# Two homes for the transposed activations, and queries asked for ahead of keys and values, in a fused sparse attention and feed-forward kernel

## The chip, the cores and the metric

The kernel runs on one core of a Trainium2 chip. The metric is device time in microseconds of one execution; before the change its median is 812.19 us over 3 runs (811.87 to 813.76).

## The reference

Block-sparse attention (4 batches, 8 heads, 768 positions, head size 64, blocks of 32) is followed by a layer norm and a feed-forward layer with a residual:

```
scores = q k^T / 8, masked by block: neighbours, first and last block, 3 sampled blocks per query block
attn   = softmax(scores) v                      (first and last query block see all keys)
x      = attn, heads side by side               (4 x 768 rows of 512)
xn     = (x - mean) / sqrt(var + 1e-6) * g
out    = x + relu(xn w1) w2                     (w1 512 x 2048, w2 2048 x 512)
```

## The kernel before

The 3072 rows are 24 tiles of 128, six for each batch, in the order t = 1, 2, 3, 0, 4, 5. Each tile with t > 0 is one job of kind N (four query blocks, each with 8 key blocks) with two visits, one for each half of the heads. Tile t = 0 holds the four edge blocks: a job H with one visit and a job D (two blocks that see all keys) with four. So a batch has 15 visits, and `s` counts the visits of the whole program.

At each step `s` the loop writes, in this order: `scores` of this visit (TensorE, line 203, into `ps`), `biggest` (VectorE, lines 236 to 239), `attn_v` and `evict` of the visit before (line 266 into `pv`, lines 295 to 312), `softmax` (ScalarE, line 246), then a list of tasks (loads for the next job, `turn` of this visit at line 256, pieces of weight preparation in the first steps, `norms`) with feed-forward matmuls spread between them by a budget (`run`). Every engine executes in the order written. There is no scheduler behind it.

The loads of the next job are written at the first visit of the present one and all go through SyncE's queue (SP), which issues in order and waits in order:

- `keys` of an N job: one DMA for the neighbour blocks (line 144, 768 KB), then twelve gathers of one sampled block each (line 153, 64 KB each), three for each of the four query blocks; D: two halves (line 134, 768 KB each). Two buffers `ks` by turns.
- `values`: lines 180 and 188 on SP (D: line 176, 1560 KB) and gathers by index on GpSimd's queue (line 192). Two buffers `vs` by turns.
- `load_q` (line 171, 256 KB): the queries of the next tile, from a table of tasks by step, so behind all of the next job's keys and values.

A matmul of `scores` for an N visit needs the tile's queries and the three gathers of its query block; the loop runs over two head pairs, and over the four blocks within each.

The rows of a tile are normed (`norm_a`: lines 319 to 327, giving the fp16 parts `xh` and `xl`), and two DMA transposes on SP (`norm_b`, lines 331 and 332) bring them into `xth` and `xtl`, from where the up projection (`ffn`, line 349 into `pu`) reads them. There is one `xth` and one `xtl`, with room for the two tiles of a unit (the first and the last unit have one tile). So a unit's transposes wait until the unit before has done its last up matmul (`up_done`). The down projection is line 373 (`pd`), its eviction line 379. In the first visits VectorE, ScalarE and GpSimd also split the weights into two fp16 parts (`split_w`, lines 402 to 413), 4 pieces a step.

Of the kernel before, what the change touches and what calls it, by code (L numbers as in the profile page):

```python
# [10 lines left out]
F16 = mybir.dt.float16  # L11
# [14 lines left out]
def sparse_attention_moe(  # L26
# [13 lines left out]
    nc = tc.nc  # L40
    P = 128
# [3 lines left out]
    CT, FT = DM // P, DF // P  # L45
# [4 lines left out]
    const = ctx.enter_context(tc.tile_pool(name="const", bufs=1))  # L50
# [6 lines left out]
    def ring(name, n, shape, dtype):  # L57
        return [const.tile(shape, dtype, name=f"{name}{i}") for i in range(n)]
# [12 lines left out]
    xn_s = const.tile([P, DM], F32, name="xn")  # L71
    xh_s = ring("xh", 2, [P, DM], F16)
    xl_s = ring("xl", 2, [P, DM], F16)
    xth = const.tile([P, CT, 2 * P], F16, name="xth")
    xtl = const.tile([P, CT, 2 * P], F16, name="xtl")
    hh_s = const.tile([P, FT * 2 * P], F16, name="hh")
    hl_s = const.tile([P, FT * 2 * P], F16, name="hl")
    ot_s = ring("ot", 2, [P, DM], F32)
# [7 lines left out]
            name=nc.get_next_instruction_name(), act_func_set_id=ACT_SET, ins=[], outs=[]  # L86
# [146 lines left out]
    def biggest(vi):  # L233
        n, w = vi.shape
        st = vi.st = sm.tile([P, 8], F32, tag="st", name=f"st{vi.i}")
        nc.vector.tensor_reduce(out=st[:, 0:n],  # L236
                                in_=vi.ps[:, 0 : n * w].rearrange("p (h k) -> p h k", k=w),
                                axis=AX.X, op=ALU.max, negate=True)
        nc.vector.tensor_scalar(out=st[:, 4 : 4 + n], in0=st[:, 0:n], scalar1=0.125,
                                scalar2=None, op0=ALU.mult)  # L240
# [75 lines left out]
    def norm_a(t):  # L316
        st = sm.tile([P, 10], F32, tag="ln", name=f"ln{t.n}")
        x, xn, xh, xl = t.x, xn_s, xh_s[t.n % 2], xl_s[t.n % 2]
        nc.vector.bn_stats(st[:, 0:6], x)
        nc.vector.bn_aggr(st[:, 6:8], st[:, 0:6])  # L320
        nc.scalar.activation(st[:, 8:9], st[:, 7:8], AF.Ln, bias=eps)
        nc.scalar.activation(st[:, 9:10], st[:, 8:9], AF.Exp, scale=-0.5)
        nc.vector.scalar_tensor_tensor(out=xn, in0=x, scalar=st[:, 6:7], in1=g_sb,
                                       op0=ALU.subtract, op1=ALU.mult)
        nc.scalar.activation(xn, xn, AF.Copy, scale=st[:, 9:10])
        nc.scalar.copy(xh, xn)
        nc.gpsimd.tensor_sub(xl, xn, xh)  # L327

    def norm_b(t):
        s = slice(t.pos * P, (t.pos + 1) * P)  # L330
        nc.sync.dma_start_transpose(out=xth[:, :, s], in_=xh_s[t.n % 2])
        nc.sync.dma_start_transpose(out=xtl[:, :, s], in_=xl_s[t.n % 2])

    def ffn(u):
        n = len(u.tiles) * P
        hh = hh_s[:, 0 : FT * n].rearrange("p (f n) -> p f n", n=n)
        hl = hl_s[:, 0 : FT * n].rearrange("p (f n) -> p f n", n=n)
        step = 512 // n
        c1 = 109 if n == 256 else 84
        for f in range(0, FT, step):  # L340
            while any((1, x // 2) not in split for x in range(f, f + step)):
                yield -1
            ph = ps_f.tile([P, 512], F32, tag="pf", name=f"pu{u.i}_{f}")
            for j in range(step):
                fs = slice((f + j) * P, (f + j + 1) * P)
                m = 0
                for w, x in ((w1h, xth), (w1l, xth), (w1h, xtl)):
                    for ct in range(CT):
                        nc.tensor.matmul(ph[:, j * n : (j + 1) * n], w[:, ct, fs], x[:, ct, 0:n],  # L349
                                         start=m == 0, stop=m == 3 * CT - 1,  # L350
                                         skip_group_check=True)
                        m += 1
                        if m < 3 * CT:
                            yield c1
                if j < step - 1:
                    yield c1
            dh = hh[:, f : f + step, :].rearrange("p f n -> p (f n)")
            dl = hl[:, f : f + step, :].rearrange("p f n -> p (f n)")
            nc.scalar.activation(dh, ph, AF.Relu)  # L359
            nc.vector.scalar_tensor_tensor(out=dl, in0=ph, scalar=0.0, in1=dh,  # L360
                                           op0=ALU.max, op1=ALU.subtract)
            if f + step == FT:
                u.up_done = True
            yield c1
        for t in u.tiles:
            ts = slice(t.pos * P, (t.pos + 1) * P)
            po = ps_f.tile([P, 512], F32, tag="pf", name=f"pd{t.n}")
            m = 0
            for f in range(FT):
                while (2, f) not in split:  # L370
                    yield -1
                for x, w in ((hh, w2h), (hl, w2h), (hh, w2l)):
                    nc.tensor.matmul(po, x[:, f, ts], w[:, f, :], start=m == 0,  # L373
                                     stop=m == 3 * FT - 1)
                    m += 1
                    if m < 3 * FT:
                        yield 215
            ot = ot_s[t.n % 2]
            nc.vector.scalar_tensor_tensor(out=ot, in0=po, scalar=1.0 / (SW1 * SW2), in1=t.x,  # L379
                                           op0=ALU.mult, op1=ALU.add)  # L380
            nc.gpsimd.dma_start(out[t.b, t.t], ot)
            t.done = True
            yield 215
# [44 lines left out]
    tiles, units, visits = [], [], []  # L428
# [5 lines left out]
    while n < len(tiles):  # L434
        k = 1 if n == 0 or n == len(tiles) - 1 else 2
        u = SimpleNamespace(i=len(units), tiles=tiles[n : n + k], up_done=False, gen=None)
# [32 lines left out]
    def at(step, fn, *args):  # L469
        todo.setdefault(step, []).append((fn, args))  # L470
# [19 lines left out]
        at(3, load_w2, i, nc.gpsimd)  # L490
    for i in range(16):
        at(4 + i // 4, split_w2, i)
    for t in tiles[1:]:
        at(tiles[t.n - 1].visits[0].i, load_q, t.n)
    for b in range(1, B):
        at(tiles[6 * b - 2].visits[0].i, load_kg, b)

    queue, nextu, s = [], 0, 0
# [14 lines left out]
    def norms():  # L513
        for t in tiles:
            if t.ready and t.normed is None and (t.n < 2 or tiles[t.n - 2].spread is not None):
                norm_a(t)
                t.normed = s
            if t.normed is not None and t.spread is None:
                if t.u.i == 0 or units[t.u.i - 1].up_done:
                    norm_b(t)  # L520
                    t.spread = s

    while s < NV + LAG + 2 or queue or nextu < len(units):
        assert s < NV + 60
        vi = visits[s] if s < NV else None
        pvi = visits[s - LAG] if 0 <= s - LAG < NV else None
        if vi:
            scores(vi)
            biggest(vi)
        if pvi:  # L530
            t = pvi.tile
            if pvi is t.visits[0]:
                assert t.n < NX or tiles[t.n - NX].done
            attn_v(pvi)
            evict(pvi)
            if pvi is t.visits[-1]:
                t.ready = True
        if vi:
            softmax(vi)
        while nextu < len(units) and units[nextu].at <= s:  # L540
            u = units[nextu]
            if any(t.spread is None or t.spread >= s for t in u.tiles):
                break
            u.gen = ffn(u)
            u.left = 192 * (84, 109)[len(u.tiles) - 1] + 48 * 215 * len(u.tiles)
            queue.append(u)
            nextu += 1
        budget = 0
        if queue:
            left = sum(u.left for u in queue)  # L550
            budget = left / (max(1, units[nextu].at - s) if nextu < len(units) else 1)
        tasks = [(fn, args) for fn, args in todo.pop(s, [])]
        if vi:
            nxt = jobs[vi.job.i + 1] if vi is vi.job.visits[0] and vi.job.i + 1 < len(jobs) else None
            pre = []
            if nxt:
                gen = keys(nxt)
                pre = [(next, (gen, 0)), (values, (nxt,))] + [(next, (gen, 0))] * 6
            tasks = pre + tasks
            if queue:  # L560
                k = len(tasks) // 2
                tasks = tasks[:k] + [(turn, (vi,))] + tasks[k:]
            else:
                tasks = [(turn, (vi,))] + tasks
        tasks.append((norms, ()))
        for fn, args in tasks:
            run(budget / (len(tasks) + 1))
            fn(*args)
        if queue:
            want = sum(u.left for u in queue) - (left - budget)  # L570
            run(want)
        norms()
        s += 1

# [50 lines left out]
```

## Time and profile before

| | |
|---|---|
| median of 3 runs | 812.19 us (811.87 to 813.76) |
| profiled execution, its own time | 817.5 us |
| its span | 815.7 us |
| TensorE busy (matmul) | 717.9 us, 88% |
| TensorE weight loads | 483.8 us, 59% |
| VectorE / ScalarE / GpSimd busy | 314.2 / 278.3 / 210.8 us |
| DMA moved | 132.16 MB, 162 GB/s over the span |

The profile's page divides the span into 40 slices of 20.4 us. TensorE is below nine tenths of each slice up to about 160 us and at 9 nearly everywhere after it. So the time before 160 us is read by what VectorE, ScalarE, GpSimd and the DMA queues do there, and the time after it by the few places in which TensorE stands still.

### The profile page before, as it was taken

The numbers are of one execution on the slowest core, as the hardware profiler recorded it, in microseconds if no ns is written. First come the engines' busy times: TensorE is split into PE (matmuls) and PEld (weight loads), VectorE is DVE, ScalarE is ACT, GpSimd is POOL, SyncE is SP. The second block draws the span as 40 slices with busy tenths as digits, with TensorE's granted clock in tenths as the row PEclk, the third lists the DMA queues.
The fourth block names the chain that finished last, engine by engine and source line by source line (L and its number), as shares of the span: only waits on it lengthen the run. The fifth ranks groups of instructions, "written<-read, shape, count | busy, mean of one in ns | idle before, by whom it ended". The sixth has DMA issues, their size and how long they took to land.

```text
span 815.7 us, 21773 instructions
## 1 busy us (share of the span) xinstructions
PE 717.9 (88%) x9344; PEld 483.8 (59%) x9344; DVE 314.2 (39%) x618; ACT 278.3 (34%) x553; POOL 210.8 (26%) x236
## 2 busy tenths in 40 slices
PE   0545565999999999999999999989999999989997
PEld 0234432675685774765774856755866846756764
DVE  2577877334242341443341432333432332342211
ACT  0356454233343341342342431343432422333200
POOL 5276547121412103023230202023321020200000
PEclk9966786799999999999999999999999999999999
DMA  8997789138938439168947367168757194261000
GB/s 332 260 322 194 279 259 248 53 89 201 259 107 223 123 103 282 32 158 224 229 97 185 99 198 207 41 161 233 215 138 185 33 277 128 70 141 40 14 27 14
DMA packets 109792, 132.16 MB, mean 162 GB/s; under 512 B 34561, under 2 KB 80897, under 8 KB 108673
## 3 DMA queue, kind: packets, MB, share of 16 engines
q1 hardware_dynamic: 96848, 83.92, 40.0%
q0 software_dynamic: 12416, 46.51, 17.7%
q8 instruction: 74, 1.21, 0.6%
q10 hardware_dynamic: 432, 0.34, 0.1%
q14 instruction: 22, 0.17, 0.1%
HBM read 118.15 MB, written 6.29 MB: 153 GB/s over the span
## 4 chain that ended last, share of the span: by engine, by line
PE 55%; issue 20%; DMA 13%; POOL 5%; SPq 4%; DVE 2%; ACT 1%; POOLq 0%
PE pu L349 24%; PE pd L373 16%; PE ps L203 7%; DMA vs<-v 6%; PE pv L266 5%; PE pt L256 4%; DMA ks<-kT 4%; SPq L153 3%; DMA q<-qT 2%; POOL w2l L413 2%; POOL vs L192 1%; DVE ot L404 1%; POOL xl L327 1%; DMA samp<-sampled 1%; POOL ks L168 0%
## 5 line engine op out<-in xcount | busy, mean ns | idle before, releaser
L246 ACT ACTIVATE p<-ps,st 128x256 f32<-128x256 f32 (+1 forms) x192 | 83.3, 510 | 273.4 <-DVE rs L295 164.8
L349 PEld LDWEIGHTS <-w1h 128*128 128x128 f16 x1664 | 152.7, 99 | 18.6 <-issue 0.3
L373 PE MATMUL pd<-w2l,hh 128*128 128x512 f16 x384 | 147.5, 384 | 8.2 <-POOL w2l L413 4.5
L373 PE MATMUL pd<-w2h,hh 128*128 128x512 f16 x384 | 147.3, 384 | 3.1 <-ACT w2h L412 3.1
L373 PE MATMUL pd<-w2h,hl 128*128 128x512 f16 x384 | 147.5, 384 | 0.0
L360 DVE SCALAR_TENSOR_TENSOR hl<-pu,hh 128x512 f16<-128x512 f32 x96 | 66.4, 692 | 181.1 <-ACT hh L359 180.2
L373 PEld LDWEIGHTS <-hh 128*128 128x128 f16 x768 | 75.4, 99 | 94.5 <-issue 13.2
L203 PE MATMUL ps<-ks,q 64*32 64x256 f32 (+1 forms) x1664 | 83.5, 420 | 47.6 <-DMA ks<-kT 26.2
L349 PE MATMUL pu<-xth,w1l 128*128 128x256 f16 (+1 forms) x832 | 120.6, 266 | 0.0
L349 PE MATMUL pu<-xth,w1h 128*128 128x256 f16 (+1 forms) x832 | 120.6, 266 | 0.0
L349 PE MATMUL pu<-xtl,w1h 128*128 128x256 f16 (+1 forms) x832 | 120.5, 265 | 0.1
L236 DVE TENSOR_REDUCE st<-ps 128x4 f32<-128x1024 f32 (+1 forms) x60 | 69.1, 1151 | 122.6 <-PE ps L203 122.6
L192 POOL DMA_INDIRECT vs<-v,rows x88 | 87.9, 998 | 99.1 <-PE pv L266 60.5
L359 ACT ACTIVATE hh<-pu 128x512 f16<-128x512 f32 x96 | 57.4, 598 | 125.0 <-PE pu L349 110.9
L256 PE MATMUL pt<-id_sb,p 128*128 128x128 f32 x448 | 67.5, 293 | 28.4 <-ACT p L246 28.4
L203 PEld LDWEIGHTS ps<-ks,q 64*32 64x32 f32 x1664 | 34.8, 110 | 85.6 <-issue 75.0
L257 ACT COPY pt<-pt 128x512 f32<-128x512 f32 x120 | 62.1, 564 | 64.7 <-PE pt L256 56.9
L349 PEld LDWEIGHTS <-w1l 128*128 128x128 f16 x832 | 78.2, 99 | 8.5
L256 PEld LDWEIGHTS pt<-id_sb,p 128*128 128x128 f32 x448 | 54.9, 149 | 40.1 <-ACT p L246 33.4
L379 DVE SCALAR_TENSOR_TENSOR ot<-pd,x 128x512 f32<-128x512 f32 x24 | 16.6, 690 | 156.5 <-PE pd L373 156.5
L266 PEld LDWEIGHTS pv<-vs,pt 128*32 128x32 f32 x3584 | 56.5, 112 | 32.9 <-issue 24.1
L266 PE MATMUL pv<-vs,pt 128*32 128x65 f32 x3584 | 67.9, 225 | 5.1 <-issue 2.9
(75 smaller groups left out, 416.4 us busy)
## 6 DMA issues: line engine op xcount, KB each, us to landing
ks<-kT SPq DMA_DIRECT2D x28, 768.0 KB
ks<-kT SPq DMA_DIRECT2D x264, 64.0 KB
vs<-v SPq DMA_DIRECT2D x20, 780.0 KB
vs<-v SPq DMA_DIRECT2D x4, 1560.0 KB
q<-qT SPq DMA_DIRECT2D x24, 256.0 KB
out<-ot POOLq DMA_DIRECT2D x24, 256.0 KB
vs<-v SPq DMA_DIRECT2D x16, 260.0 KB
w2h<-w POOLq DMA_DIRECT2D x4, 1024.0 KB
```

Of the source, the lines that this page charges most:

```text
L153: nc.sync.dma_start(kv[:, gg, r, :], src[:, bass.ds(reg[NR * gg + r], 1), :] .rearrange("p o e -> p (o e)"))
L192: nc.gpsimd.indirect_dma_start(out=vs[:, 2 * gg, :], out_offset=None, in_=src, in_offset=bass.IndirectOffsetOnAxis(ap=rows[:, i : i + 1], ...
L203: nc.tensor.matmul(ps[32 * part : 32 * part + 32, col : col + n], lhs[64 * row : 64 * row + 64], rhs[64 * row : 64 * row + 64], start=True ...
L236: nc.vector.tensor_reduce(out=st[:, 0:n], in_=vi.ps[:, 0 : n * w].rearrange("p (h k) -> p h k", k=w), axis=AX.X, op=ALU.max, negate=True)
L246: nc.scalar.activation(p_s[:, hs], vi.ps[:, hs], AF.Exp, bias=vi.st[:, 4 + h : 5 + h], scale=0.125)
L256: nc.tensor.transpose(pt[:, k - lo, :], p_s[:, k * P : (k + 1) * P], id_sb)
L257: nc.scalar.copy(dst[:, lo:hi, :], pt[:, 0 : hi - lo, :])
L266: nc.tensor.matmul(pv[32 * row : 32 * row + 32, 65 * col : 65 * col + 65], pt[:, ch, 32 * row : 32 * row + 32], vs[:, vv, 65 * e : 65 * e ...
L349: nc.tensor.matmul(ph[:, j * n : (j + 1) * n], w[:, ct, fs], x[:, ct, 0:n], start=m == 0, stop=m == 3 * CT - 1, skip_group_check=True)
L359: nc.scalar.activation(dh, ph, AF.Relu)
L360: nc.vector.scalar_tensor_tensor(out=dl, in0=ph, scalar=0.0, in1=dh, op0=ALU.max, op1=ALU.subtract)
L373: nc.tensor.matmul(po, x[:, f, ts], w[:, f, :], start=m == 0, stop=m == 3 * FT - 1)
```

## The change

Three things change. `xth` and `xtl` become two each, used by turns of the unit. The condition on a tile's transposes is relaxed accordingly: they are written once the unit two before (no longer the one before) has done its up matmuls. And `load_q` leaves the table of tasks: it is written ahead of the next job's keys and values, when that job is the first of its tile.

```
-    xth = const.tile([P, CT, 2 * P], F16, name="xth")
-    xtl = const.tile([P, CT, 2 * P], F16, name="xtl")
+    xth_s = ring("xth", 2, [P, CT, 2 * P], F16)
+    xtl_s = ring("xtl", 2, [P, CT, 2 * P], F16)
...
-        nc.sync.dma_start_transpose(out=xth[:, :, s], in_=xh_s[t.n % 2])
-        nc.sync.dma_start_transpose(out=xtl[:, :, s], in_=xl_s[t.n % 2])
+        nc.sync.dma_start_transpose(out=xth_s[t.u.i % 2][:, :, s], in_=xh_s[t.n % 2])
+        nc.sync.dma_start_transpose(out=xtl_s[t.u.i % 2][:, :, s], in_=xl_s[t.n % 2])
...
     def ffn(u):
         n = len(u.tiles) * P
+        xth, xtl = xth_s[u.i % 2], xtl_s[u.i % 2]
...
-    for t in tiles[1:]:
-        at(tiles[t.n - 1].visits[0].i, load_q, t.n)
...
-                if t.u.i == 0 or units[t.u.i - 1].up_done:
+                if t.u.i < 2 or units[t.u.i - 2].up_done:
...
-                pre = [(next, (gen, 0)), (values, (nxt,))] + [(next, (gen, 0))] * 6
+                pre = [(load_q, (nxt.visits[0].tile.n,))] if nxt.visits[0] is nxt.visits[0].tile.visits[0] else []
+                pre += [(next, (gen, 0)), (values, (nxt,))] + [(next, (gen, 0))] * 6
```

Where it moves instructions is seen on SP. `DMAHW` names are the eight semaphores that SP's DMAs use by turns; a wait on PE, Activation or Pool is one on a compute engine. First, SP between the H job's loads and the next N job's in the third batch, about 455 to 487 us in the trace. Before:

```order
L171 DMA q1_89<-qT 128x512 [waits DMAHW6_49]
L331 DMA_TRANSPOSE xth_100<-xh1_97 128x4x128 [waits DMAHW7_49,PE_49,Activation_49]
L332 DMA_TRANSPOSE xtl_101<-xl1_99 128x4x128 [waits DMAHW0_49,PE_49,Pool_49]
L134 DMA ks0_79<-kT 128x1536 [waits DMAHW1_49]
L176 DMA vs0_83<-v2 128x6x520 [waits DMASW7_49,DMASW6_49,DMAHW2_49,DMASW5_49,PE_49]
L134 DMA ks0_79<-kT 128x1536 [waits DMAHW3_49]
L171 DMA q0_88<-qT 128x512 [waits DMAHW4_49]
L331 DMA_TRANSPOSE xth_100<-xh0_96 128x4x128 [waits DMAHW5_49,Activation_49]
L332 DMA_TRANSPOSE xtl_101<-xl0_98 128x4x128 [waits DMAHW6_49,Pool_49]
L144 DMA ks1_80<-kT 128x4x384 [waits DMAHW7_49]
```

Now:

```order
L331 DMA_TRANSPOSE xth1_101<-xh1_97 128x4x128 [waits DMAHW7_49,Activation_49]
L332 DMA_TRANSPOSE xtl1_103<-xl1_99 128x4x128 [waits DMAHW0_49,Pool_49]
L134 DMA ks0_79<-kT 128x1536 [waits DMAHW1_49,PE_49]
L176 DMA vs0_83<-v2 128x6x520 [waits DMASW7_49,DMASW6_49,DMAHW2_49,DMASW5_49,PE_49]
L134 DMA ks0_79<-kT 128x1536 [waits DMAHW3_49]
L331 DMA_TRANSPOSE xth1_101<-xh0_96 128x4x128 [waits DMAHW4_49,Activation_49]
L332 DMA_TRANSPOSE xtl1_103<-xl0_98 128x4x128 [waits DMAHW5_49,Pool_49]
L171 DMA q0_88<-qT 128x512 [waits DMAHW6_49]
L144 DMA ks1_80<-kT 128x4x384 [waits DMAHW7_49]
```

The transposes stand where they stood, but the first pair no longer waits for TensorE; the D job's keys behind them now carry that wait, for an older visit's scores. The query load has moved behind the second pair, directly ahead of its own tile's keys.

Second, SP at the end of that same kind of round, after the twelve gathers of one N job and before the loads of the next (about 370 us in the trace). Before:

```order
L171 DMA q1_89<-qT 128x512 [waits DMAHW3_49]
L161 DMA kg0_81<-kT 128x2x128 [waits DMAHW4_49]
L331 DMA_TRANSPOSE xth_100<-xh1_97 128x4x128 [waits DMAHW5_49,PE_49,Activation_49]
L332 DMA_TRANSPOSE xtl_101<-xl1_99 128x4x128 [waits DMAHW6_49,PE_49,Pool_49]
L144 DMA ks0_79<-kT 128x4x384 [waits DMAHW7_49,PE_49]
L180 DMA vs0_83<-v2 96x4x520 [waits DMAHW0_49,PE_49]
L188 DMA vs0_83<-v2 32x4x520 [waits DMAHW1_49]
```

Now:

```order
L161 DMA kg0_81<-kT 128x2x128 [waits DMAHW4_49]
L331 DMA_TRANSPOSE xth1_101<-xh1_97 128x4x128 [waits DMAHW5_49,Activation_49]
L332 DMA_TRANSPOSE xtl1_103<-xl1_99 128x4x128 [waits DMAHW6_49,Pool_49]
L171 DMA q0_88<-qT 128x512 [waits DMAHW7_49,PE_49]
L144 DMA ks0_79<-kT 128x4x384 [waits DMAHW0_49]
L180 DMA vs0_83<-v2 96x4x520 [waits DMAHW1_49,PE_49]
L188 DMA vs0_83<-v2 32x4x520 [waits DMAHW2_49]
```

The queries of the coming tile (`q1_89`) are gone from here: they went out ahead of its keys, one round earlier. Those of the tile after it (`q0_88`) stand ahead of line 144 instead of behind the next twelve gathers.

Third, SP in the first batch, ahead of the first D job (about 82 to 110 us). Before:

```order
L171 DMA q1_89<-qT 128x512 [waits DMAHW0_49]
L134 DMA ks0_79<-kT 128x1536 [waits DMAHW1_49,PE_49]
L176 DMA vs0_83<-v0 128x6x520 [waits DMASW2_49,DMASW1_49,DMAHW2_49,DMASW0_49,PE_49]
L134 DMA ks0_79<-kT 128x1536 [waits DMAHW3_49]
L171 DMA q0_88<-qT 128x512 [waits DMAHW4_49]
L331 DMA_TRANSPOSE xth_100<-xh1_97 128x4x128 [waits DMAHW5_49,PE_49,Activation_49]
L332 DMA_TRANSPOSE xtl_101<-xl1_99 128x4x128 [waits DMAHW6_49,PE_49,Pool_49]
```

Now:

```order
L331 DMA_TRANSPOSE xth1_101<-xh1_97 128x4x128 [waits DMAHW1_49,Activation_49]
L332 DMA_TRANSPOSE xtl1_103<-xl1_99 128x4x128 [waits DMAHW2_49,Pool_49]
L134 DMA ks0_79<-kT 128x1536 [waits DMAHW3_49,PE_49]
L176 DMA vs0_83<-v0 128x6x520 [waits DMASW2_49,DMASW1_49,DMAHW4_49,DMASW0_49,PE_49]
L134 DMA ks0_79<-kT 128x1536 [waits DMAHW5_49]
```

Here, and only here, a pair of transposes has come ahead of loads that it used to follow.

ScalarE executes in the same order. On TensorE a few `turn` and `scores` groups of the H and D visits move by 2 to 5 down matmuls. On VectorE and GpSimd, once in each of the last three batches, the eviction and store of a finished down projection come ahead of a tile's norm instead of behind it.

## Rows read from the trace of the kernel before

**Rows 1.** The page: span, and TensorE's busy tenths in 40 slices.

```profile
span 815.7 us, 21773 instructions
...
PE   0545565999999999999999999989999999989997
```

**Rows 2.** Windows: length, busy us of PE, PEld, DVE, ACT, POOL, granted clock, DMA share, GB/s.

```profile
40.00:60.00 20.00, 10.46 (x200) 7.61 (x200) 15.31 (x17) 10.69 (x17) 14.24 (x12) 0.60 0.91 318
...
100.00:120.00 20.00, 13.16 (x183) 8.46 (x185) 13.89 (x24) 10.97 (x21) 8.82 (x10) 0.82 0.82 245
...
380.00:400.00 20.00, 18.29 (x276) 11.46 (x275) 4.81 (x11) 6.29 (x15) 10.18 (x12) 1.00 0.95 243
...
480.00:500.00 20.00, 19.55 (x167) 9.93 (x166) 3.04 (x9) 4.57 (x9) 6.76 (x8) 1.00 1.09 325
```

**Rows 3.** Waits: engine and line, what for, us in total, times, longest us.

```profile
PE ps L203 <- DMA q<-qT: 16.6, 5, 8.1
```

**Rows 4.** Timeline of TensorE, scores of N visits: start, us, then idle before and releaser.

```profile
50.01 2.30 PE L203 MATMUL ps<-ks,q 64*32 64x256 f32 x32 [8.06 <-DMA q<-qT]
...
72.72 2.29 PE L203 MATMUL ps<-ks,q 64*32 64x256 f32 x32 [4.18 <-DMA q<-qT]
...
196.45 1.43 PE L203 MATMUL ps<-ks,q 64*32 64x256 f32 x32 [1.19 <-issue]
...
372.90 1.52 PE L203 MATMUL ps<-ks,q 64*32 64x256 f32 x32 [1.14 <-DMA q<-qT]
...
393.00 1.43 PE L203 MATMUL ps<-ks,q 64*32 64x256 f32 x32 [1.21 <-DMA q<-qT]
...
529.03 1.09 PE L203 MATMUL ps<-ks,q 64*32 64x256 f32 x32
...
551.10 1.52 PE L203 MATMUL ps<-ks,q 64*32 64x256 f32 x32 [2.04 <-DMA q<-qT]
...
728.56 1.52 PE L203 MATMUL ps<-ks,q 64*32 64x256 f32 x32 [1.87 <-issue]
```

**Rows 5.** Timeline of TensorE: first D visits of three batches, and an H step's attn_v.

```profile
311.10 1.49 PE L203 MATMUL ps<-ks,q 64*32 64x512 f32 x16 [1.29 <-DVE ot L379]
...
475.51 1.11 PE L266 MATMUL pv<-vs,pt 128*32 128x65 f32 x64
...
488.42 1.49 PE L203 MATMUL ps<-ks,q 64*32 64x512 f32 x16 [0.46 <-DMA ks<-kT]
...
666.47 1.50 PE L203 MATMUL ps<-ks,q 64*32 64x512 f32 x16 [1.20 <-DMA ks<-kT]
```

**Rows 6.** Chain that ended last: start, us from issue to landing, transfer.

```profile
369.80 2.86 DMA q<-qT
...
477.95 10.33 DMA ks<-kT
...
677.84 3.34 DMA ks<-kT
```

**Rows 7.** SP's own waits, the one on line 331.

```profile
SPq L331 <- PE pu L349: 110.6, 8, 28.9
```

**Rows 8.** Timeline of SP, third batch: last H query load, transposes, D values.

```profile
454.95 1.31 SPq L171 DMA_DIRECT2D q<-qT  x1
474.19 1.22 SPq L331 DMA_TRANSPOSE xth<-xh  x1
...
477.52 0.38 SPq L176 DMA_DIRECT2D vs<-v  x1
```

**Rows 9.** Timeline of GpSimd: the step that makes xl, first and third batch.

```profile
95.54 1.15 POOL L327 TENSOR_TENSOR xl<-xn,xh 128x512 f16<-128x512 f32 x1
...
462.95 1.15 POOL L327 TENSOR_TENSOR xl<-xn,xh 128x512 f16<-128x512 f32 x1 [10.30 <-ACT xh L326]
```

**Rows 10.** Timeline of VectorE: row maxima of the visits at 50 and 73 us.

```profile
52.34 1.22 DVE L236 TENSOR_REDUCE st<-ps 128x4 f32<-128x1024 f32 x1 [4.11 <-PE ps L203]
...
75.06 1.23 DVE L236 TENSOR_REDUCE st<-ps 128x4 f32<-128x1024 f32 x1 [1.82 <-PE ps L203]
```

## Prediction

> **What bounds the kernel now.** I read the page first, to find the stretches with different limits, then the windows, then TensorE's waits by line, then TensorE's timeline at each of those waits, and last SP's queue and the chain of waits, to see what landed late and why. The page's slices show two stretches [rows 1]: until about 160 us TensorE is far from full; after it, TensorE is full but for short stops. In the first stretch the other engines and the DMA queues are busy: between 40 and 60 us VectorE works 15.3 us of 20 and the DMA share is 0.91 [rows 2]. In the second, an idle microsecond of TensorE is a microsecond of the kernel, unless the same transfer makes it wait again soon after. So I look for idle time of TensorE after 160 us, and for idle time of VectorE before it.
>
> TensorE waited 16.6 us in five places for the query load alone [rows 3]; two more such places are put down to "issue". They are the first visits of N tiles: at 50.01 and 72.72 us in the first stretch, at 196.45, 372.90, 393.00, 551.10 and 728.56 in the second [rows 4]. The reason is the place of the load in SP's queue: it is the last of the tile's transfers. At 369.80 it is issued after twelve gathers, lands 2.86 us later [rows 6], and the scores start 0.24 us after that [rows 4]. The second kind of stop is the first visit of a D job, 1.29, 0.46 and 1.20 us [rows 5]. There the D keys come late because SP stands on a pair of transposes that waits for the up projection of the unit before: nothing is issued from 454.95 to 474.19 [rows 8], and line 331 waited 110.6 us for TensorE in 8 places [rows 7]. The three D-job stops are the ones where a late load stands behind such a wait.
>
> **The sum, term by term.**
>
> Term A, queries first, after 160 us. Nothing is added or taken away: 24 query loads move ahead of their tile's keys and values, and the gathers are issued about when they were, since the values load ahead of them still waits for TensorE. What must land last is now the twelfth gather. The five stops cost 1.19 + 1.14 + 1.21 + 2.04 + 1.87 = 7.45 us idle, and the visits after them run 1.43 to 1.52 us where an undisturbed one runs 1.09, together 7.42 - 5 x 1.09 = 1.97 more [rows 4]. So 9.42 us is the ceiling. The floor comes from the gather's landing. A gather issued into a crowded queue at 677.84 landed in 3.34 us, against the query load's 2.86, and it is issued some 0.4 us (one issue) sooner [rows 6], so it may land no earlier than the queries did. Even then TensorE gains: the loop over four query blocks runs twice, and the last block's keys are first needed after 6 of 16 groups. What is left after the landing is 10/16 of 1.09 to 1.52, that is 0.68 to 0.95 us, where all of 1.52 was left: at least 0.55 us a stop. I take 1.0 a stop, between 0.55 and the 1.6 to 2.4 of single stops, since it is nearest to the row with the shorter flight, 2.86. The stops at 372.90 and 393.00 hang on one run of transfers with a DMA share of 0.95 [rows 2], so they don't add up: the second gains what the first did, and 256 KB that no longer lie in that run, 0.8 us at 325 GB/s. That is 1.8 us for both. With 1.0 at 196.45, 1.5 at 551.10 (a weaker second stop follows it) and 1.0 at 728.56, A is 5.3 us; bounds 2.2 (four independent places x 0.55) and 9.4.
>
> Term B, transposes no longer waiting, after 160 us. In the third batch the pair can go when the tile's `xl` is made, 462.95 + 1.15 = 464.1 [rows 9], instead of 474.19. The first half of the D keys, 768 KB, then goes at about 467. The D values wait for the H step's attn_v, 475.51 + 1.11 = 476.6, 0.9 us before they now go [rows 5, 8], and the second half goes behind them. So 2328 KB instead of 3096 KB lie between 477 and D's scores. The second half now takes 10.33 us from issue to landing [rows 6]; three quarters of that is 7.8, landing at about 485, and the scores are due at 488. All three stops go: 2.95 us. I take 2.8; bounds 0 (the D1 stop at 311.10 is put down to VectorE, and the others may be) and 2.95. The other waits of line 331 are worth nothing: no stop follows them. What gets later: in the last three batches the next tile's pair now stands behind the eviction of a down projection that ends about when D's scores start (488.42), not close behind the H step (476.6) [rows 5], and SP's loads of the next N tile stand behind that pair: up to 12 us later. Their first reader is the visit at 529.03 [rows 4], 40 us on: cover enough, and if it were gone the price would be up to those 12 us a batch.
>
> Term C, before 160 us. VectorE's chain of weight splits and row maxima sets the pace there. It idles 4.11 us for the scores at 50 us and 1.82 us for those at 73 [rows 10]. At 50 us the clock is 0.60 of full [rows 2] and the scores take 2.30; with queries first 10/16 of them, 1.4, is left after the last landing, which saves 0.9, and up to 0.4 for the earlier issue. The next job's values go out behind that visit's attn_v, so its saving is passed on; at 73 us the same 1.3 is saved again, and VectorE's idle 1.82 covers it. That is 2.6 at most by this reckoning, 3.5 if the landings come earlier. Against it stands the one place where transposes have come ahead of loads: the first D keys, now behind `xl` at 95.54 + 1.15 [rows 9]. 768 KB move into a stretch with 245 GB/s at a share of 0.82 [rows 2], which can cost up to 3.1 us or, with that room, nothing. I take C as 2.0; bounds -3.1 and 3.5.
>
> Sum: 5.3 + 2.8 + 2.0 = 10.1 us. The profiled execution took 817.5 us, so 807.4; it is 5.3 us above the median of 812.19, on which the same gain gives **802.1 us**. With all ceilings it is 812.2 - 15.9 = 796.3.
>
> **The rivals.**
>
> Queue-bound: the order in the queue is indifferent. For it speaks the share of 0.95 between 380 and 400 us [rows 2]: if the queue is full, the last byte lands when it did, whichever transfer it belongs to, and a bunch of gathers arriving together leaves no part of a visit to run ahead. A and C are then nothing, B stays: 812.2 - 2.9 = 809.3 us. Against it speaks the load at 369.80, which took 2.86 us for 256 KB: that is a short flight, not a queue. The Trainium skill has this rule ("DMA: Bandwidth & Descriptors", Two DMAs through the same engine are not ordered: descriptors within one queue of an engine start in order but are pipelined); the row at 369.80 agrees only in part, since SP's issue and not the queue sets the time there.
>
> Nothing moves: the transposes stand in SP's queue where they stood, only their wait is gone, and SP meets the next wait of the same time (for `xl`, for the older visit's scores, for attn_v). With the gathers landing as late as the queries did, each stop stays under another name: 812 us. Against it: the waits that come next are over 10 us (464.1) and 0.9 us (476.6) earlier by the rows above.
>
> Slower: the first D keys, behind the transposes of tile 1, arrive after their visit is due. The row maximum of that visit then comes late, VectorE's last four weight splits stand behind it, and TensorE's full stretch begins later. The price is 3.1 us of transfer, and if A and B gave nothing the kernel would take 812.2 + 3.1 = 815.3. It decides only where A and B fail together, since their floors of 2.2 and 2.9 outweigh it; the share of 0.82 speaks against it too.
>
> **How the numbers follow.** The forecast, A to C at about these sizes, has a chance of 0.74; queue-bound 0.13; nothing moves 0.07; slower 0.06. A measurement of this kernel can tell about 0.3%, 2.4 us, from no change. The forecast is faster by more than that, and so is the queue-bound case in most of its width (I give 0.1 of 0.13 to faster): faster 0.84, same 0.10, slower 0.06. The range goes from the ceilings, 796, to the queue-bound case, 809.5; it leaves out the last two rivals and a little of the others.
>
> **What would show each step.** TensorE's waits by line should have no entry "ps from DMA q" of more than 1 us after the first visits; what is left of the stops should be put down to `ks`. The first D visits should start without idle time, with the first half of the D keys issued about 10 us ahead of the D values. SP's line 331 should wait for ScalarE or GpSimd and no longer for TensorE. VectorE's row maxima near 50 and 73 us should come 1 to 3 us sooner, and TensorE's full stretch should begin about 2 us sooner. The prediction is wrong if the stops in the N tiles keep their 1 to 2 us with `ks` as the releaser, if a new stop appears at the N tile after a D job, or if the D visit of the first batch waits for its keys.

## The result, and the profile after

The changed kernel takes 798.69 us (median of 6 runs, 798.03 to 799.43), the kernel before, run beside it, 812.21 (809.59 to 813.76). The ratio is 0.9837, with a 95 % interval of 0.9821 to 0.9852: 13.5 us faster. On two more chips the same pair gave 0.988 (0.9854 to 0.9907) and 0.9854 (0.9815 to 0.9894), so about 11 us there. The forecast was 802.1, the range 796.0 to 809.5.

The page of the profiled execution after: span, and TensorE's busy tenths in 40 slices.

```profile
span 796.1 us, 21782 instructions
...
PE   0476474899999999999999999999999999999997
```

The slices with 8 after 160 us [rows 1] are gone. TensorE's waits show why. These are the two entries that its scores (line 203) have left: engine, line, what for, us in total, times, longest.

```profile
PE ps L203 <- DMA ks<-kT: 30.1, 7, 22.7
...
PE ps L203 <- issue: 0.5, 2, 0.2
```

There is no entry for the query load, which stood with 16.6 us [rows 3]; the keys stand with 30.1 us where they had 26.2 before, so some 4 of the 16.6 came back as waits for keys. From line 334 on the numbers of the changed kernel are one higher. The next rows are TensorE's timeline after (start, us): the first visits of the N tiles that had stopped [rows 4] (x32), and of the D jobs [rows 5] (x16).

```profile
194.04 1.09 PE L203 MATMUL ps<-ks,q 64*32 64x256 f32 x32
...
306.76 1.49 PE L203 MATMUL ps<-ks,q 64*32 64x512 f32 x16
...
365.69 1.09 PE L203 MATMUL ps<-ks,q 64*32 64x256 f32 x32
...
382.95 1.35 PE L203 MATMUL ps<-ks,q 64*32 64x256 f32 x32
...
478.21 1.50 PE L203 MATMUL ps<-ks,q 64*32 64x512 f32 x16
...
537.13 1.09 PE L203 MATMUL ps<-ks,q 64*32 64x256 f32 x32
...
650.91 1.49 PE L203 MATMUL ps<-ks,q 64*32 64x512 f32 x16
...
709.40 1.09 PE L203 MATMUL ps<-ks,q 64*32 64x256 f32 x32
```

A row without a bracket had no idle time ahead of it. Four of the five N visits run their undisturbed 1.09 us, and no D visit waits. SP's queue around the third batch's D job, with its waits at line 331:

```profile
452.76 2.08 SPq L331 DMA_TRANSPOSE xth<-xh  x1
454.94 1.21 SPq L332 DMA_TRANSPOSE xtl<-xl  x1
456.24 0.53 SPq L134 DMA_DIRECT2D ks<-kT  x1
466.55 0.39 SPq L176 DMA_DIRECT2D vs<-v  x1
466.99 0.53 SPq L134 DMA_DIRECT2D ks<-kT  x1
```

```profile
SPq L331 <- ACT p L246: 86.2, 9, 21.4
...
SPq L331 <- ACT hh L360: 46.1, 4, 23.9
```

The first half of the D keys goes out 10.3 us ahead of the D values (it stood behind a pair at 474.19 [rows 8]), and line 331 no longer waits for TensorE, as it did for 110.6 us [rows 7].

**A part of the difference that the prediction had no term for.** By their profiles the two kernels differ by 815.7 - 796.1 = 19.6 us, 6 more than by their medians. The starts and ends of the 60 visits' scores can be set side by side in the two timelines. The surplus begins in four places that the prediction did not list, between the first and the second visit of the N tile behind each D job, 1.22 us each. These rows are of the kernel before, at the second of them: attn_v (L266), the instructions that wait for its end (L180 on SP, L295 on VectorE), and TensorE's next stop.

```profile
352.74 0.89 PE L266 MATMUL pv<-vs,pt 128*32 128x65 f32 x48
...
356.90 0.34 SPq L180 DMA_DIRECT2D vs<-v  x1
356.90 0.16 DVE L295 TENSOR_SCALAR rs<-pv 128x1 f32<-128x1 f32 x1 [2.56 <-PE pu L349]
...
359.06 0.38 PE L373 MATMUL pd<-w2l,hh 128*128 128x512 f16 x1 [0.96 <-issue]
```

And after:

```profile
347.97 0.89 PE L266 MATMUL pv<-vs,pt 128*32 128x65 f32 x48
...
349.25 0.33 SPq L180 DMA_DIRECT2D vs<-v  x1
...
349.48 0.15 DVE L295 TENSOR_SCALAR rs<-pv 128x1 f32<-128x1 f32 x1
```

attn_v ended at 353.63 (TensorE's ends are modelled in these profiles), and the two engines that wait for that started 3.27 us later; in the changed kernel it is 0.39 and 0.62 us. TensorE then stopped with nothing shown as the reason, and the next tile's values went out 3 us late. I call this the late signal. Whether it belongs to the program was the first question.

### The profile page after: what moved, and what is told of

Its sections match the earlier page's. It is cut to its first block, busy times and chain, and to the rows that moved or that the text cites. A ratio compares the mean times of both kernels' runs of the same rounds, so it can differ in the third digit from the quotient of the medians.

```text
span 796.1 us, 21782 instructions
## 1 busy us (share of the span) xinstructions
PE 717.8 (90%) x9344; PEld 480.2 (60%) x9344; DVE 314.2 (39%) x618; ACT 279.2 (35%) x553; POOL 210.3 (26%) x236
## 4 chain that ended last, share of the span: by engine, by line
PE 45%; issue 35%; POOL 9%; DMA 8%; DVE 2%; SPq 1%; ACT 1%; POOLq 0%
PE pu L350 16%; PE pd L374 16%; PE ps L203 5%; PE pv L266 4%; POOL vs L192 4%; DMA vs<-v 3%; PE pt L256 3%; DMA ks<-kT 3%; POOL w2l L414 2%; POOL xl L327 1%; POOL ks L168 1%; DVE ot L405 1%; POOL out L382 1%; SPq L153 1%; DMA samp<-sampled 1%
## 5 line engine op out<-in xcount | busy, mean ns | idle before, releaser
L203 PE MATMUL ps<-ks,q 64*32 64x256 f32 (+1 forms) x1664 | 87.8, 424 | 30.6 <-DMA ks<-kT 30.1
L382 POOL DMA_DIRECT2D out<-ot x24 | 14.0, 582 | 255.1 <-DVE ot L380 253.4
L380 DVE SCALAR_TENSOR_TENSOR ot<-pd,x 128x512 f32<-128x512 f32 x24 | 16.6, 690 | 159.6 <-PE pd L374 159.6
L203 PEld LDWEIGHTS ps<-ks,q 64*32 64x32 f32 x1664 | 31.7, 110 | 75.2 <-issue 59.4
L266 PEld LDWEIGHTS pv<-vs,pt 128*32 128x32 f32 x3584 | 55.8, 112 | 29.4 <-issue 23.1
```

The lines of the kernel that those rows point to most:

```text
L203: nc.tensor.matmul(ps[32 * part : 32 * part + 32, col : col + n], lhs[64 * row : 64 * row + 64], rhs[64 * row : 64 * row + 64], start=True ...
L266: nc.tensor.matmul(pv[32 * row : 32 * row + 32, 65 * col : 65 * col + 65], pt[:, ch, 32 * row : 32 * row + 32], vs[:, vv, 65 * e : 65 * e ...
```

## The experiments

**First four, on a second chip: the kernel before again, and each part alone.** Queries first alone leaves `xth` and `xtl` with one home each:

```diff
-    for t in tiles[1:]:
-        at(tiles[t.n - 1].visits[0].i, load_q, t.n)
...
-                pre = [(next, (gen, 0)), (values, (nxt,))] + [(next, (gen, 0))] * 6
+                pre = [(load_q, (nxt.visits[0].tile.n,))] if nxt.visits[0] is nxt.visits[0].tile.visits[0] else []
+                pre += [(next, (gen, 0)), (values, (nxt,))] + [(next, (gen, 0))] * 6
```

Two homes alone is the rest of the change. Two homes with the old place takes one line of that back:

```diff
-                if t.u.i < 2 or units[t.u.i - 2].up_done:
+                if t.u.i == 0 or units[t.u.i - 1].up_done:
```

The kernel before, again:

> The kernel before, unchanged, profiled a second time. In its first profile four stops stood that the prediction did not list: in the N tile right behind each D job (from 175.2, 351.7, 529.0 and 707.1 us) SP's values load (L180) and VectorE's L295 saw the end of TensorE's attn_v some 3.2 us late, and TensorE then idled about 0.96 us with nothing shown as the reason. Theory 1, the stop belongs to the program before: the second profile has all four again, of about 1.2 us each, and a span near 815. Theory 2, it belongs to that one execution: none or other ones, and a span near 810, 5 us less (4 x 1.22 = 4.9 us is close to the 5.3 us by which that execution lay over the median). If theory 2 holds and the N stops behind it (372.90, 551.10, 728.56) shrink too, the late values load had made part of them.

Queries first alone:

> The queries' move alone: the load ahead of keys and values, one home for the transposed tile as before. By term A as predicted 812.2 - 5.3 = 806.9 us (bounds 802.8 to 810.0); by the steps read off the two profiles (11.3 to 12 us in seven first visits) 800.5 to 801. If theory 2 on the late signal holds, the two medians' difference of 13.5 us less 3 for the D stops leaves 10.5, so 801.7. The rival, that a tile's last byte lands when it did whatever goes first, gives 812 and first visits that wait as long for keys as they had for queries. The D stops (1.3, 0.5, 1.2 us) and line 331's waits for TensorE should stand as before.

Two homes alone:

> The two homes alone: queries last in the queue as before, transposes no longer waiting for the up projection two tiles back. By term B 812.2 - 2.8 = 809.4 us (bounds 809.2 to 812.2). If the four stops behind the D jobs belong to the program before and come from the wait of SP on TensorE's last up-projection matmuls, they go too: 4.9 us more, 804.5, and the profile has no late signal at those places. The waits for the query queue (16.6 us in five places) should stand as before, within 2 us, or be smaller by what a values load that is issued 3 us sooner gives.

Two homes, old place:

> Two homes, queries last as before, and the transposes issued under the old condition. In SP's order this differs from two homes alone in one place: tile 1's pair stands behind the first D job's transfers, not ahead of its keys. If the new place costs something there (the rival of the prediction: up to 3.1 us in the stretch before 160 us), this is faster than two homes alone by up to 3.1 us; if the cover holds, as the forecast has it, the two agree within 0.5 us.

Measured: before 819.91 us (22 runs, 816.05 to 824.88), queries first 811.27 (ratio 0.9896, 0.9873 to 0.9920), two homes 816.31 (0.9956, 0.9936 to 0.9976), two homes with the old place 816.15 (0.9953, 0.9933 to 0.9972). All four profiles have the late signal, 3.3 us once and 4.1 otherwise, in the four places behind the D jobs. For the kernel before that is theory 1, so far. But two homes alone was expected to lose it if SP's wait made it, and did not: SP no longer waits for TensorE there. The last two kernels agree, 0.16 us apart. The ratio of queries first is worth 8.4 us of 812.2, between the 5.3 of term A and the 10.5 to 12 that had been expected from the two profiles; two of the three D stops stay in it, at 0.26 and 0.90 us, and one is gone, where all three had been expected to stay. Two homes alone keeps its waits for the queries, 10.2 us against 11.5 in the kernel before on that chip. It also ends the D stops; its first D visits in the last three batches have no idle time:

```profile
312.65 1.49 PE L203 MATMUL ps<-ks,q 64*32 64x512 f32 x16
...
488.95 1.49 PE L203 MATMUL ps<-ks,q 64*32 64x512 f32 x16
...
664.76 1.50 PE L203 MATMUL ps<-ks,q 64*32 64x512 f32 x16
```

**Next four, on a third chip: the changed kernel again, two variants of its start-up, and one try at the late signal.** The fourth tile's query load (tile 3) back behind its job's gathers:

```diff
+                lq = [(load_q, (nxt.visits[0].tile.n,))] if nxt.visits[0] is nxt.visits[0].tile.visits[0] else []
+                pre = [(next, (gen, 0)), (values, (nxt,))] + [(next, (gen, 0))] * 6
+                pre = pre + lq if nxt.i == 3 else lq + pre
```

The old place of the transposes is the one-line edit above, made in the changed kernel. Turned gathers, made in queries first alone:

```diff
-        for gg, i in enumerate(job.blocks):
+        late = (2, 1, 0, 3) if job.i and jobs[job.i - 1].kind == "D" else range(n)
+        for gg in late:
+            i = job.blocks[gg]
```

The changed kernel:

> The changed kernel, unchanged, timed and profiled beside the others on this chip. The two parts alone gave 0.9896 and 0.9956 of the time before, 0.985 together if they add up, that is 808 where before takes 820 and 800 where it takes 812. Theory 1, the signal that reaches VectorE and SP late behind each D job (3.3 or 4.1 us after attn_v's end in before, in queries first alone and in two homes alone, 4 times each) is gone only where both parts are made: the profile has 0.6 us in those four places again, and the ratio is 0.984 or lower. Theory 2, its absence was a matter of that one execution or chip: 3.3 to 4.1 us in the four places, TensorE stopped there for 1.2 us each, and a ratio near 0.989.

Tile 3's queries last:

> The changed kernel with one load back in its old place: the first batch's query load of the fourth tile goes behind the gathers of its H job, not ahead of them. In the changed kernel this load goes out at 72.6 us, 4.5 us ahead of the first weight load of the second matrix, for which VectorE then waited 1.95 us where it had waited 0.60. Theory, this load is what ate the start-up gain: VectorE's wait at that place falls below 0.8 us and the visits from 100 us on come 0.5 to 1.3 us sooner than in the changed kernel. Rival, the weight load's landing varies by as much from run to run (queries first alone has the same order and waited 0.18 there): no difference beyond 0.5 us, or one that does not follow the wait.

The old place:

> The changed kernel with the old condition for issuing the transposes: on every queue that differs from the changed kernel in one place, tile 1's pair, which stands behind the first D job's transfers again. In queries first alone, where the pair stands there too, the visits from 157 us on come 1.4 us sooner than in the changed kernel; between two homes alone with the new and the old place the profiles differ by 0.6 us. Theory, the new place costs 0.6 to 1.4 us of start-up (the first D keys go out 15 us later, and move in a stretch where the weights are loaded): this is 0.6 to 1.4 us faster than the changed kernel. Rival, the start-up merely varies by that much: the same within 0.5 us.

Turned gathers:

> Queries first alone, with the four value gathers of the job behind each D job in the order 2, 1, 0, 3, so that the first of them is issued when attn_v's last chunk but one is done, not while attn_v runs (the first gather went out 0.3 us ahead of attn_v's end). Theory, the late signal behind the D jobs comes from a gather that GpSimd starts while that attn_v is still running: its 4.06 us in four places fall to about 0.6, the 1.1 us stops go, and the span is some 4 us below that of queries first alone (808.6). Rival, the gathers have no part in it: 3.3 to 4.1 us again and the span within 1 us of 808.6.

Measured: before 810.53 us (11 runs), the changed kernel 799.45 (0.988, 0.9854 to 0.9907), tile 3's queries last 798.98 (0.9894, 0.9861 to 0.9928), the old place 799.42 (0.988, 0.985 to 0.991), turned gathers 797.58 (one run). The late signal is 0.6 us in all four profiles. Turned gathers lies 12.8 us of span below queries first alone (795.8 against 808.6), where 4 were expected: it looked as if the order of four gathers were worth as much as the whole change. But the two had run on different chips, and the kernel before differed between these by 9.4 us. So this showed nothing yet.

So the signal is on time, as theory 1 has it, but the ratio of the changed kernel, 0.988, is that of theory 2, and it lies outside the interval of the first pair (0.9821 to 0.9852).

The two start-up variants are the same as the changed kernel in time. The first theory falls by its own sign too. VectorE's first split of the second matrix, in the changed kernel on this chip and with tile 3's queries last:

```profile
82.54 0.90 DVE L403 TENSOR_SCALAR ot<-hh 128x512 int32<-128x512 int32 x1 [2.26 <-DMA hh<-w]
```

```profile
81.45 0.89 DVE L403 TENSOR_SCALAR ot<-hh 128x512 int32<-128x512 int32 x1 [2.27 <-DMA hh<-w]
```

The wait is the same, so that query load does not cause it. The visits from 100 us on did come sooner in that one profile, by 2.3 us (100.06 against 102.37), but 1.0 of that already stands at the second visit (33.66 against 34.67), ahead of anything the edit moves, and the medians are 0.47 us apart.

**Last four, side by side on a fourth chip.** They are copies of kernels above, without an edit: before, queries first alone, the same with turned gathers, and the changed kernel.

> The kernel before, profiled a third time, beside the three kernels that follow, all on one chip. The late signal behind the D jobs stood in every profile taken on two chips of before, queries first alone and two homes alone, and in none taken on a third chip of the changed kernel and of queries first with turned gathers. So either the program decides (theory 1: before has it here too, 3.3 to 4.1 us in four places, whatever the chip), or the chip does (theory 2: the four kernels of this chip all have it or none has it).

> Queries first alone, again, on the chip of the other three. Theory 1 (the program decides): late signals of 4.06 us in four places, stops of 1.5 us there, a values load 3.4 us late in the four tiles that follow, and 6 to 12 us more than the changed kernel. Theory 2 (the chip decides): the same late signals in this kernel, in the changed one and in before, or in none; where none, this stands within 1 to 4 us of the changed kernel, the 3 us of the D stops among them.

> Queries first with the value gathers behind the D jobs in the order 2, 1, 0, 3, again. Theory 1 with the gathers as its cause: 0.6 us in the four places although queries first alone has 4.1 here, and 6 to 12 us faster than it. Theory 2: the signals as in queries first alone, and the time within 1 us of it.

> The changed kernel on the same chip. Theory 1: 0.6 us in the four places, 0.984 of the time before or lower. Theory 2: signals as in the other three; with late ones its ratio is that of the two parts added, 0.985 (0.9896 times 0.9956), and without them it is near the 0.988 of the chip that showed none.

| on one chip | us, median | ratio (95 %) | span of the profile |
|---|---|---|---|
| before (11 runs) | 810.38 | | 808.0 |
| queries first alone | 801.13 | 0.9880 (0.9844 to 0.9916) | 798.3 |
| the same, gathers turned | 799.78 | 0.9861 (0.9826 to 0.9896) | 797.8 |
| the changed kernel | 799.13 | 0.9854 (0.9815 to 0.9894) | 795.9 |

Here no kernel has the late signal. The kernel before, at the same place in the program as above:

```profile
351.37 0.89 PE L266 MATMUL pv<-vs,pt 128*32 128x65 f32 x48
...
352.66 0.34 SPq L180 DMA_DIRECT2D vs<-v  x1
...
352.88 0.15 DVE L295 TENSOR_SCALAR rs<-pv 128x1 f32<-128x1 f32 x1
```

That is theory 2. The program before runs with the signal and without it, and turned gathers has no part in it: without the signal it lies 1.35 us from queries first alone, with intervals that overlap. On each of these three chips the four kernels have it together or not at all. No variant is faster than the changed kernel beyond its interval.

The same set shows what each part does, free of the late signal. These rows are the stops of over 0.8 us that the kernel before has here ahead of scores, after 160 us:

```profile
213.92 1.43 PE L203 MATMUL ps<-ks,q 64*32 64x256 f32 x32 [0.83 <-DVE ot L379]
...
309.73 1.49 PE L203 MATMUL ps<-ks,q 64*32 64x512 f32 x16 [0.85 <-DVE ot L379]
...
389.19 1.43 PE L203 MATMUL ps<-ks,q 64*32 64x256 f32 x32 [1.97 <-DMA q<-qT]
...
484.96 1.49 PE L203 MATMUL ps<-ks,q 64*32 64x512 f32 x16 [0.82 <-DVE ot L379]
...
564.39 1.43 PE L203 MATMUL ps<-ks,q 64*32 64x256 f32 x32 [1.65 <-DMA ks<-kT]
...
660.37 1.49 PE L203 MATMUL ps<-ks,q 64*32 64x512 f32 x16 [1.03 <-DMA ks<-kT]
...
720.91 1.52 PE L203 MATMUL ps<-ks,q 64*32 64x256 f32 x32 [1.54 <-issue]
```

In queries first alone these of over 0.5 us are left:

```profile
306.05 1.49 PE L203 MATMUL ps<-ks,q 64*32 64x512 f32 x16 [0.65 <-DVE ot L379]
...
478.47 1.49 PE L203 MATMUL ps<-ks,q 64*32 64x512 f32 x16 [0.62 <-DMA ks<-kT]
...
557.06 1.05 PE L203 MATMUL ps<-ks,q 64*32 64x256 f32 x20 [1.16 <-DMA ks<-kT]
...
653.10 1.49 PE L203 MATMUL ps<-ks,q 64*32 64x512 f32 x16 [0.88 <-DMA ks<-kT]
```

And in the changed kernel:

```profile
554.99 1.77 PE L203 MATMUL ps<-ks,q 64*32 64x256 f32 x24 [0.55 <-DMA ks<-kT]
```

The N stops go with the queries but for the one at 557.06, which the second home halves; the D stops go only with the second home. All fourteen profiles bear that out: in the seven kernels with the second home no first D visit of the last three batches has idle time ahead of it, in the seven without it two or three of them have, 0.18 to 1.29 us. On this chip queries first alone gained 7.4 us after the start-up, and the second home 3.2 more, of which 2.4 lie at the D jobs.

## Why the prediction was right

By the gain of the visits' ends on the last chip, before against changed:

| term | predicted | measured | where |
|---|---|---|---|
| A, queries first, after 160 us | 5.3 (2.2 to 9.4) | 7.65 | 0.52 + 1.09 + 0.80 + 1.93 + 1.09 + 0.18 + 2.04, seven first visits of N tiles |
| B, no wait of the transposes | 2.8 (0 to 2.95) | 2.9 | 0.91 + 0.90 + 1.11, three D jobs |
| C, start-up | 2.0 (-3.1 to 3.5) | 1.6 here, -0.07 in the pair of the record, 0.5 on average | up to the third D visit of the first batch |
| sum | 10.1 | 12.2 | spans 808.0 - 795.9 = 12.1; medians 11.25 |

The forecast of 802.1 was 3.4 us above the measured 798.69. A was 2.4 us too small on the last chip and C 0.4 to 2.1 too large; that the two offset each other is luck.

**Term A was right in its mechanism and too small.** (23 query loads moved, not 24: the first tile's was ahead already.) The step that failed is the landing of the last gather: "it may land no earlier than the queries did", from a flight of 3.34 us [rows 6] and an issue 0.4 us sooner. SP's queue in the fourth batch on the last chip, before and then changed:

```profile
703.30 0.34 SPq L180 DMA_DIRECT2D vs<-v  x1
703.69 2.78 SPq L188 DMA_DIRECT2D vs<-v  x2
709.19 8.51 SPq L153 DMA_DIRECT2D ks<-kT  x12
717.75 0.42 SPq L171 DMA_DIRECT2D q<-qT  x1
```

```profile
693.15 0.33 SPq L180 DMA_DIRECT2D vs<-v  x1
693.53 1.75 SPq L188 DMA_DIRECT2D vs<-v  x2
698.00 8.48 SPq L153 DMA_DIRECT2D ks<-kT  x12
```

```profile
709.15 1.09 PE L203 MATMUL ps<-ks,q 64*32 64x256 f32 x32
```

From the values load to the end of the last issue SP took 718.17 - 703.30 = 14.9 us before, the query load's own 0.4 included, and 706.48 - 693.15 = 13.3 after: 1.5 us sooner, not 0.4. The gathers themselves, "issued about when they were" by the prediction, ended 1.1 us sooner after the values load, and 1.0 of that lies in line 188 (2.78 us against 1.75). The last row is the visit's scores: they start 2.7 us after the last issue and run without a stop. The last block's keys are needed 6/16 of the way in, 0.4 us later, so the last gather landed within some 3.1 us (an estimate from these rows), less than the 3.34 of the floor. The visit at 720.91 gains its whole stop: 1.54 idle and 0.43 of slow scores are 1.97, and 2.04 was gained. I had taken 1.0. One stop stays, the visit at 554.99, where 0.18 of a stop of 1.65 was gained. The five places that the prediction listed gave 0.52 + 0.80 + 1.93 + 1.09 + 2.04 = 6.38 of the 7.65, against 5.3; the other 1.27 came in two visits, 213.92 and 564.39, that had no such stop in the profile from which it was reckoned.

**Term B** came out as reckoned. In the kernel before's time (10.12 us later at that point) the changed kernel of the record issues the first half of the D keys at 466.4 and the D values at 476.7; the prediction had 467 and 476.6. Of the 2.9 us, 0.56 came with the queries alone on the last chip and 2.36 with the second home. With the queries first and one home the D stops stay at 0.65, 0.62 and 0.88 us, so they are not the queries' alone; with two homes and the queries last they are gone. Two of them are put down to VectorE on the last chip, which had made me keep 0 as a bound. They went all the same, and not because that eviction came sooner: in the changed kernel it is still under way when the first D visit starts at 305.99, and that visit has no idle time.

```profile
305.66 0.69 DVE L380 SCALAR_TENSOR_TENSOR ot<-pd,x 128x512 f32<-128x512 f32 x1 [10.02 <-PE pd L374]
```

So the scores do not need that eviction, and the keys are what is left to have ended the stops.

**Term C was too large, because a load that the prediction did not count holds VectorE back.** The third D visit of the first batch, about where TensorE's full stretch begins (by the slices of [rows 1] it is at 9 from 143 us on, not from 160), starts in the kernel before at 157.21, 157.99 and 158.48 us in three profiles; in queries first alone (two of them with turned gathers) at 155.88, 156.10, 156.15 and 156.82; in the changed kernel at 157.28, 158.20 and 156.84. On average that is 157.9, 156.2 and 157.4. In the pair of the record it begins no sooner at all, where 2 us were expected. The row maxima near 50 and 73 us did come sooner, by 0.96 and 1.19 us in that pair and by 0.06 and 2.78 on the last chip. Then VectorE waits for the first piece of the second matrix, which GpSimd loads behind its own part of the first one's splits. These rows are that load's issue and the split that needs it, on the last chip, before and then changed:

```profile
77.14 0.58 POOL L397 DMA_DIRECT2D hh<-w  x1
...
82.89 0.43 DVE L402 TENSOR_SCALAR ot<-hh 128x512 int32<-128x512 int32 x1
```

```profile
77.03 0.58 POOL L398 DMA_DIRECT2D hh<-w  x1
...
81.55 0.65 DVE L403 TENSOR_SCALAR ot<-hh 128x512 int32<-128x512 int32 x1 [2.63 <-DMA hh<-w]
```

Of the 2.78 us 1.1 is left when this split ends. The issue does not move with the queries: it stands at 77.02 to 77.62 us in thirteen of the fourteen profiles and at 78.39 in the other. In eleven of them VectorE waits for this load, which came 3.7 to 6.6 us after its issue, and in those eleven the third D visit starts 73.5 to 74.8 us after the split's end, whatever the kernel. What makes the load land sooner or later is open.

The place of tile 1's pair of transposes, which the "slower" rival named, is not shown to cost anything. With the pair in its old place the changed kernel starts that visit at 156.83, and two homes alone at 158.22 in place of 158.80; but with tile 3's queries last, where the pair stands in the new place, it starts at 155.86, the earliest of all. Counted from the end of the split, the mean is 74.1 us for the four profiles with queries first and the new place and 73.95 for the seven others that wait. The medians of the two pairs that differ in the place alone lie 0.03 and 0.16 us apart.

**The sum** was formed against the median, 5.3 us below the profiled execution of before. That was right, for a reason I did not know, as far as the profiles of the last chip show it; the runs of before beside the changed kernel have no profile that shows it. The profile without late signals has 7.7 us less than the 815.7 of that span: 4 x 1.22 = 4.9 us of stops behind D jobs, 3.8 in the N stops that follow, where values and gathers were issued late, 0.3 in the D stops, and 1.3 the other way at the start. The 13.5 us of the record are more than the 12.2 of the clean pair; its ratio, 0.9837, lies inside the interval of that pair. What makes up the rest is not shown.

**The rivals.** Queue-bound would have given queries first alone nothing; it gave 9.25 us by the medians of the last chip. The rule of the Trainium skill named there ("DMA: Bandwidth & Descriptors", Two DMAs through the same engine are not ordered) says that descriptors of one queue of an engine start in order but are pipelined; the rows agree as far as they go, since the queries that were issued first never ended a wait. Nothing moves: the waits for queries and for transposes are gone, and what stays under another name is one stop of 0.55 us. Slower: the first D visit of the first batch had no wait for its keys, and C, at -0.07 us in the pair of the record and 1.6 on the last chip, never came near -3.1. (The prediction let floors of 2.2 and 2.9 outweigh this rival; its own floor for B was 0.) The prediction named as a sign of failure that "a new stop appears at the N tile after a D job"; there was a stop, but in the profile of before.

## What to carry to other kernels

Where several transfers must land for one step, put the one large transfer that can be issued early ahead of the many small ones whose issue sets the time; here most of the seven first visits gained their whole stop by it, and one stop of 1.65 us only 0.18. Before counting time saved on one engine, look for the next transfer that it waits for: here a load issued by another engine took back more than half of what the start-up had gained. A second buffer pays where a queue that issues in order stands on the first one, and only as much as the stops of the loads behind it. Compare variants that ran side by side on one chip: the same kernel differed by 9.5 us between two, as much as the whole change, and a profile of one execution can carry stops that its program does not have.

## What the runs showed that I had not expected

On the second chip, and in the first profile of before, TensorE's signal for the end of one attn_v in 15 visits reached SP and VectorE 3.3 or 4.1 us after the modelled end, where 0.4 to 0.6 is usual, always at the last D visit of a batch, and TensorE then stopped (0.96 us above; 0.43 and 0.79 in queries first alone on the second chip). Since the end is modelled, the profiles do not tell a late signal from an attn_v that itself ended late. In windows of 1 us the granted clock was 1.00 with the late signal and without it, and the DMA share was 0.00 in before from 349 to 354 us, up to the moment when the signal was due; in the changed kernel it was 0.00 there as well. The same program ran with it (815.7 and 815.1 us of span) and without it (808.0). What makes it is open. The runs tie it to the chip or to the execution, not to either part of the change. The first profile of before took 817.5 us, above all six timed runs beside the changed kernel (809.59 to 813.76) and inside the range of the second chip (816.05 to 824.88); on which chip it ran is not on record.
